# Strassen's first output and the gate's mix accumulated in PSUM, in a gated mix of linear attention and a Mish layer

## The chip, the cores and the metric

The kernel runs on one core of a Trainium2 chip. A core has five engines with a queue each: TensorE (PE in the profile, its weight loads PEld) multiplies matrices into PSUM, VectorE (DVE), ScalarE (ACT) and GpSimd (POOL) work on tiles, and SyncE (SP) issues most of the DMAs. SBUF is the working memory of 128 partitions; PSUM has eight banks of 128 x 512 fp32 values, which the code names by three tags: "a" (three banks), "dn" (four) and "kv" (one). The metric is the device time of one execution in microseconds (us), the median of the runs.

## The reference

For x of 2048 rows and 512 columns it computes g * a + (1 - g) * b, with one gate g per row:

```python
g = sigmoid((x * gate_w).sum(-1, keepdims=True))
# a: q, k, v = x @ wqkv, 32 heads of 16
pq, pk = q @ w_phi, k @ w_phi                       # per head
phi = concat([softmax(p), softmax(-p)])             # of pq and of pk
kv, z = phi_k^T v, sum over rows of phi_k
a = (phi_q kv) / (phi_q z + 1e-6), heads joined, @ wo
# b: a dense layer with Mish
h = x @ w1 + b1
b = (h * tanh(softplus(h))) @ w2                    # 512 -> 1376 -> 512
```

All is fp32. The kernel multiplies in the type fp32r; each factor is split into a high part h and a rest l, and a product is h*h + h*l + l*h, so three matmuls stand for one.

## The kernel before, in words

**Stage A** (names A0 to A7) goes over eight chunks of 256 rows. It makes the k features (k0, k1 on TensorE; mx, mn, d0, d1, S, rS, ml on VectorE; E, the exponential, on ScalarE), sums kv and z, and makes q and v. For chunks 1 to 7, q and v come from Strassen's scheme in Winograd's form, with seven products p1 to p7 of six matmuls each in place of eight. **Stage S** makes the hidden layer: S0 for the row blocks 0 and 1, S1 for 2 and 3. Hidden columns are taken in five pairs of 128 (the digit behind the underscore is the pair's), and each pair is again seven products p1 to p7 over the two row blocks. **Stage B** (B0 to B3, 512 rows each) multiplies by w2 (dn0 to dn10, each a sweep of 12 matmuls over four row tiles), makes the q features, the numerator (nu), the product with wo (wo0 to wo3), and the mix.

**In a seven-product group**, p1 and p2 sum to the first output, and p1, p6, p7, p4 go one after the other into the same bank (`d["a"]`, `ps["a"]`), with a ScalarE copy of the bank between them where an output needs the sum so far: c1 after p1, c6 after p6. p2 has a bank of its own (`d["c"]`, `ps["c"]`), and a VectorE addition a2 adds that bank to c1's copy in SBUF (lines 423 and 740). p5 and p3 go into a third bank, which c5 copies. In stage S the sums then go through Mish on ScalarE (mA0, mA1, mB0, mB1); those of the first row block stay in SBUF, those of the second are stored to DRAM and read back (sB, la).

**The mix** of a row tile: for even blocks ScalarE scales the finished sweep (iz, out of the bank "dn" into SBUF), and VectorE adds g times the product with wo (fi, line 1058). For odd blocks ScalarE scales the product with wo (ag) and VectorE adds the sweep.

**What sets the order.** The text RUN is a list of step names written out by hand. It is run from left to right, and every instruction is pinned, so each engine's queue holds its instructions in that order. An engine takes its queue in order: an instruction that waits holds up all behind it. SyncE's queue of DMAs is such a queue too. Buffers rotate by tag: the n-th tile of a tag gets buffer n modulo the number of buffers, and waits until that buffer's last reader is done.

**The low parts** are subtractions of raw and high part: on GpSimd for sl (line 368), wd (line 700), the rest of wo (WL, line 586), most of x (line 628), the h of the sweeps (line 824) and w2 (gl, line 559). gh (ScalarE) makes the high part of a pair's w2 blocks from raw tiles that lg loads.

Of the kernel before, what the change touches and what calls it, by code (L numbers as in the profile page):

```python
# [8 lines left out]
F32 = mybir.dt.float32  # L9
# [31 lines left out]

RUN = """
    A0.mx0 A0.mx1 A0.xh A0.xl A0.v0 A0.mn1 A0.mn0 A0.fq A0.fh2 S0.l11 A0.d10 A0.tA0 A0.fh1 A0.v1 A0.tA1 A0.tH1 A0.fl1 A0.tB1 A0.tB0 A0.fl2 A1.p1
    A0.ve1 A0.d11 A0.tH2 A0.fh0 A0.fl0 A0.d00 A0.d01 A0.tL1 A0.tL2 A0.fh3 A0.fl3 A0.E0 A0.E1 A2.lx A0.tC3 A0.tC4 A0.tH4 A1.k0 A1.mn0 A0.q0 A0.qe0
    A1.su A1.c1 A1.mx0 A1.d10 A1.ldx A0.tH3 A1.p2 A1.d00 A0.S1 A0.S0 A1.E0 A1.S0 A0.ldx A0.tL4 A0.q1 A1.xh A1.xl A1.k1 A1.mx1 A0.rS1 S0.l21 A1.rS0
    A0.qe1 A2.p1 A0.rS0 A0.tL3 A1.sh A2.k0 A1.ml0 A2.k1 A1.d01 A0.ml0 A1.a2 A2.p2 A1.sl A1.p6 A2.su A1.mn1 A1.d11 A0.ve0 A1.E1 A2.xh A0.ml1 A2.xl
    A0.st0 A0.st1 A0.z1 A1.c6 A0.z0 A1.z0 S0.h21 A2.c1 A1.p5 A0.kv A1.c5 A1.S1 A1.rS1 A1.p7 A1.p3 A2.sh A2.sl A3.su A2.mn0 A1.ml1 A1.a7 A2.mx1 A1.st1
    A3.k1 A2.a2 A1.a3 A2.mx0 A2.d10 A2.d00 A3.p1 A2.E0 A2.S0 A3.ldx A2.rS0 A1.z1 S0.wr_0 A2.p6 A2.c6 A2.ldx A2.p5 A2.c5 A2.p7 A1.p4 A2.d01 A2.mn1
    A2.d11 A2.E1 A2.p3 A3.sh S0.wa_0 A2.ml0 A1.st0 A3.mn1 A3.c1 A3.k0 A2.a3 A2.z0 A2.st0 A3.sl A3.p5 A2.a7 A2.p4 A1.e4 A3.xh A2.S1 A3.mx0 A3.mx1
    A3.mn0 A1.kv A3.xl S0.l12 A2.e4 A2.rS1 A2.ml1 A2.kv A3.d00 A3.d10 A3.E0 S0.wb_0 S0.ws_0 A3.p6 A4.p1 A2.z1 A3.d11 A3.S0 A3.rS0 A3.ml0 A2.st1 A2.wx  # L50
    A3.c5 A4.k0 A4.mn0 A3.c6 A4.su A3.p3 A4.d10 A3.a3 A4.c1 A3.p7 A4.sh A4.mx0 S0.h11 A4.d00 A3.a7 A4.k1 A4.E0 A3.st1 A3.d01 A4.mn1 A4.d11 A4.S0 A4.sl
    A3.p2 A3.a2 A4.mx1 A4.p5 A4.p6 A3.z0 A3.E1 A4.xh A4.c6 A4.ldx A3.S1 A3.rS1 A4.p2 A4.p7 A4.d01 A4.c5 A3.ml1 A3.p4 A4.a7 A4.st1 A4.E1 A3.st0 S0.o11
    A4.xl A4.rS0 A4.ml0 A4.p3 A5.su A5.sh A4.a3 A3.z1 S0.t1 A3.e4 B0.lq0 A5.k0 A5.k1 A5.mx0 A4.S1 A4.z0 A4.rS1 A4.ml1 A5.sl S0.h1 S0.o1 A4.z1 S0.o21
    A5.xh A5.p1 A5.c1 A3.kv A5.p5 A5.c5 A4.st0 A4.a2 A5.mn0 A5.p6 A5.mx1 A5.xl A5.d01 S0.wc_0 A5.mn1 A5.d10 A5.d11 A5.d00 A5.E0 A4.p4 A5.S0 A5.rS0
    A5.p3 A6.p1 A5.E1 A6.su A5.c6 A5.ml0 A5.z0 B0.mx0 A5.a3 A4.e4 A5.p7 A6.sh A6.sl A5.S1 A5.rS1 A4.kv B0.mn0 A5.ml1 A5.ldx A6.xh A6.k0 A6.mn0 A6.mx0
    A5.a7 A6.d00 A6.d10 A6.k1 A6.mn1 A6.mx1 A6.E0 A5.p2 A5.st0 A5.z1 A6.S0 A6.c1 A6.p2 A6.a2 S0.l22 A5.p4 A6.d01 A5.st1 A6.p6 A6.d11 A6.p5 A6.xl
    A6.rS0 A6.ml0 A6.c6 A6.p7 A7.su A6.E1 A6.S1 A6.c5 A6.p3 A5.e4 S0.t2 A6.z0 S0.fr0 A5.a2 A6.rS1 A7.p1 A6.a7 A7.p2 A7.sh A6.zr A7.sl A6.st1 A6.p4
    A6.ml1 S0.h2 S0.t3 S0.fh0 S0.t4 A7.k0 S0.h22 A6.z1 S0.fl0 S0.o22 A6.e4 A7.mn0 A6.a3 A5.kv A6.kv A7.c1 S0.lg1 A7.d10 A7.mx0 A7.d00 B0.d00 A6.zm
    S0.o2 A7.p5 A7.E0 A7.S0 A7.rS0 A6.st0 A7.c5 A7.k1 A7.mx1 A7.mn1 S0.gh1 S0.gl1 S0.wr_1 S0.h3 S0.p1_0 A7.d01 A7.p6 A7.c6 A7.d11 A7.p3 A7.ml0 A7.E1
# [47 lines left out]
def tile_gated_mix(ctx: ExitStack, tc: tile.TileContext, xT, wv, wkT, wqT, bd, w1a, w1b, b1, w2a, w2b, wo, out):  # L107
# [8 lines left out]

    def mm(*a, **k):
        return pin(nc.tensor.matmul(*a, **k))  # L118

    def T(shape, dt, tag, bufs, name):  # L120
        nm[0] += 1
        return sp.tile(shape, dt, name=f"{name}_{nm[0]}", tag=tag, bufs=bufs)
# [23 lines left out]
    def f32(ap):  # L146
        return ap.bitcast(F32)
# [1087 lines left out]
```

## Time and profile before

| what | value |
|---|---|
| median of 3 runs | 430.3 us (429.46 to 431.18) |
| the profiled execution, first to last instruction | 431.1 us |
| the slowest of the three runs | 431.18 us |
| TensorE (PE) busy | 422.3 us, 98% |
| VectorE (DVE) busy | 369.3 us, 86% |
| ScalarE (ACT) busy | 253.6 us, 59% |
| GpSimd (POOL) busy | 263.6 us, 61% |
| mean granted TensorE clock | 0.996 |

A busy time is the union of an engine's instructions. Matmuls are pipelined: one of 128x512 lasts 389 ns in the records, but the next starts 227 ns after it, so PE's busy share alone doesn't tell how close TensorE is to its pace. In a row of the timeline the first number is the start in us from the span's start, the second the duration, and a bracket at the end tells how long the engine had been idle and what ended that. L118 and L138 are the helpers through which every matmul and nearly every ScalarE instruction is recorded, so groups are told apart by tiles.

### The profile page before, as it was taken

The numbers are of one execution on the slowest core, as the hardware profiler recorded it, in microseconds if no ns is written. First come the engines' busy times: TensorE is split into PE (matmuls) and PEld (weight loads), VectorE is DVE, ScalarE is ACT, GpSimd is POOL, SyncE is SP. The second block draws the span as 40 slices with busy tenths as digits, with TensorE's granted clock in tenths as the row PEclk, the third lists the DMA queues.
The fourth block names the chain that finished last, engine by engine and source line by source line (L and its number), as shares of the span: only waits on it lengthen the run. The fifth ranks groups of instructions, "written<-read, shape, count | busy, mean of one in ns | idle before, by whom it ended". The sixth has DMA issues, their size and how long they took to land. (4 is left out here: it accounts for less than half of the span.)

```text
span 431.1 us, 7558 instructions
## 1 busy us (share of the span) xinstructions
PE 422.3 (98%) x2772; PEld 340.2 (79%) x2772; DVE 369.3 (86%) x519; ACT 253.6 (59%) x373; POOL 263.6 (61%) x186
## 2 busy tenths in 40 slices
PE   8999999999998999899999999999999999999996
PEld 7888888888886877688878687788788887877875
DVE  3899789998998999998999998799989699999512
ACT  3574463646254899768679813467978467851131
POOL 2298868799674966635666494977455627541220
PEclk9999999999999999989999999999999999999999
DMA  7900597675988344433888477833533725555532
GB/s 260 366 34 28 164 273 182 140 179 126 209 171 214 108 134 123 160 109 122 235 249 281 165 239 237 281 91 122 177 119 143 232 73 188 179 199 168 197 121 75
DMA packets 52670, 74.06 MB, mean 172 GB/s; under 512 B 8085, under 2 KB 32149, under 8 KB 52633
## 3 DMA queue, kind: packets, MB, share of 16 engines
q1 hardware_dynamic: 50440, 66.36, 47.9%
q0 software_dynamic: 1904, 6.82, 9.5%
q8 instruction: 22, 0.36, 0.3%
q10 hardware_dynamic: 288, 0.39, 0.3%
q14 instruction: 16, 0.12, 0.1%
HBM read 43.53 MB, written 28.85 MB: 168 GB/s over the span
## 5 line engine op out<-in xcount | busy, mean ns | idle before, releaser
L118 PE MATMUL down<-w2g,h 128*128 128x512 f32 x316 | 98.5, 393 | 0.0
L118 PEld LDWEIGHTS down<-w2g,h 128*128 128x128 f32 x316 | 58.6, 188 | 14.8 <-issue 2.5
L118 PE MATMUL down<-w2g,l 128*128 128x512 f32 x158 | 61.8, 391 | 0.2 <-POOL l L824 0.2
L824 POOL TENSOR_TENSOR l<-act,h 128x512 fp32r<-128x512 f32 (+1 forms) x24 | 32.3, 1345 | 41.2 <-ACT h L138 16.7
L824 POOL TENSOR_TENSOR l<-actb,h 128x512 fp32r<-128x512 f32 x20 | 29.0, 1451 | 38.3 <-ACT h L138 20.7
L138 ACT ACTIVATE E<-E 128x1024 f32<-128x1024 f32 x32 | 33.4, 1057 | 16.5 <-DVE E L285 7.1
L118 PE MATMUL up<-x,w1sh 128*128 128x512 f32 x144 | 39.7, 397 | 2.2 <-DVE act L740 2.1
L118 PE MATMUL wo<-woh,ohl 128*128 128x512 f32 x128 | 40.9, 389 | 0.0
L118 PEld LDWEIGHTS down<-w2g,l 128*128 128x128 f32 x158 | 29.6, 188 | 7.5 <-POOL l L824 1.2
L118 PEld LDWEIGHTS up<-x,w1sh 128*128 128x128 f32 x144 | 26.7, 189 | 9.2 <-DVE act L740 2.5
L700 POOL TENSOR_TENSOR w1sl<-w1r,w1sh 128x1024 fp32r<-128x1024 f32 x9 | 22.2, 2467 | 18.0 <-ACT w1sh L138 17.4
L118 PE MATMUL proj<-tw,sx 128*128 128x512 f32 x126 | 31.5, 394 | 1.5 <-ACT qs L138 1.5
L628 POOL TENSOR_TENSOR x<-xr,x 128x1024 fp32r<-128x1024 f32 x10 | 26.7, 2666 | 3.6 <-ACT x L138 3.6
L118 PEld LDWEIGHTS proj<-tw,sx 128*128 128x128 f32 x126 | 23.3, 188 | 6.9 <-ACT qs L138 1.9
L138 ACT ACT_TABLE_LOAD x22 | 28.2, 1283 | 0.4
L118 PEld LDWEIGHTS wo<-woh,ohl 128*128 128x128 f32 x128 | 24.0, 188 | 5.0
L138 ACT ACTIVATE act<-act,b1s 128x512 f32<-128x512 f32 x30 | 21.4, 719 | 10.9 <-DVE act L740 4.1
L118 PE MATMUL up<-x,w1d 128*128 128x512 f32 x108 | 27.7, 398 | 0.0
L267 POOL TENSOR_TENSOR xl<-xraw,xh 128x512 fp32r<-128x512 f32 x14 | 18.3, 1370 | 15.3 <-ACT xh L138 15.0
L138 ACT ACTIVATE act<-up 128x512 f32<-128x512 f32 x30 | 17.6, 590 | 16.8 <-PE up L118 16.4
L138 ACT ACTIVATE h<-actb 128x512 fp32r<-128x512 f32 x20 | 12.4, 628 | 24.4 <-DMA actb<-ab 18.9
L118 PE MATMUL wo<-wol,ohl 128*128 128x512 f32 x64 | 24.9, 389 | 0.0
(173 smaller groups left out, 1086.4 us busy)
## 6 DMA issues: line engine op xcount, KB each, us to landing
ed<-E SPq DMA_DIRECT2D x16, 512.0 KB, 3.1
eT<-ed SPq DMA_DIRECT2D x64, 128.0 KB, 3.2
za<-E POOLq DMA_DIRECT2D x11, 512.0 KB, 6.8
xr<-in_xT_dram SPq DMA_DIRECT2D x20, 256.0 KB, 4.2
ab<-act SPq DMA_DIRECT2D x20, 256.0 KB, 2.9
actb<-ab SPq DMA_DIRECT2D x20, 256.0 KB, 3.3
pqd<-qs SPq DMA_DIRECT2D x16, 256.0 KB, 5.8
pq<-pqd SPq DMA_DIRECT2D x16, 256.0 KB, 3.6
```

The source lines that it names most:

```text
L118: return pin(nc.tensor.matmul(*a, **k))
L138: return pin(A_.activation(out_, in_, fn, **k))
L267: pin(eng.tensor_sub(xs[c][1][j], kt(rawx[c], SC)[:, 2 * j : 2 * j + 2, :], f32(xs[c][0][j])))
L628: pin((V if n in LOV else G_).tensor_sub(X[n][:, 1024:], xr[n], f32(X[n][:, :1024])))
L700: pin(G_.tensor_sub(W["sl"], W["r"], f32(W["sh"])))
L824: pin(G_.tensor_sub(U[i]["l"][:n, :], U[i]["a"][:n, :], f32(U[i]["h"][:n, :])))
```

## The change

1. **p2 is added in PSUM.** c1 now copies bank a to bank c, PSUM to PSUM, on ScalarE, and p2 accumulates onto it. The VectorE addition a2 is gone. In stage A a new ScalarE step e2 takes v out of bank c; in stage S Mish reads bank c directly.
2. **The mix is summed in PSUM** for blocks 0 to 2: iz scales the sweep from its "dn" bank into the bank of the product with wo, wo accumulates on it, and fi is a ScalarE copy to SBUF. g is multiplied into the q features' scale instead (sc). Block 3 keeps the old way with VectorE.
3. **The split wo** and the split w1 block of the gate's column are stored to DRAM once (WS, fs) and read back for S1 (and, for the w1 block, also for the second row block), in place of a new load, ScalarE copy and GpSimd subtraction.
4. **GpSimd's subtractions of 1024 columns** are two of 512 (low).
5. **RUN is another order,** and SLOTS gives each tile of most tags a buffer by number in place of the rotation.

The number of matmuls of each shape is the same.

```diff
+SLOTS = {
+    "a": (
+        "012001021202102101201021012212010202121010210212020210110211202101010101"
+    ),
...
+    def home(tag, bufs):
+        return (tag + next(homes[tag]), 1) if tag in homes else (tag, bufs)
...
+    def low(l, a, h):
+        for o in range(0, 1024, 512):
+            pin(G_.tensor_sub(l[:, o : o + 512], a[:, o : o + 512], f32(h[:, o : o + 512])))
...
-                    mm(acc[r // 64][c : c + 64, o : o + 64], staged[r : r + 64, k, G, c : c + 64], bds[r : r + 64, G, r : r + 64], start=True, stop=True, skip_group_check=True)
+                    mm(acc[r // 64][c : c + 64, o : o + 64], staged[r : r + 64, k, G, c : c + 64], bds[r : r + 64, G, r : r + 64], start=(fresh and G == 0), stop=True, skip_group_check=True)
...
         def sl():
-            pin(G_.tensor_sub(sx["t"][:, 1024:], rawx[c][:, :], f32(sx["t"][:, :1024])))
+            low(sx["t"][:, 1024:], rawx[c][:, :], sx["t"][:, :1024])
...
         def p2():
-            d["c"] = psum("proj", "dn")
-            product(d["c"], xq(0, 1), B((wvh, wvl), 1), True)
+            product(d["c"], xq(0, 1), B((wvh, wvl), 1))
...
         def c1():
-            vs[c, 0] = k2("v", "io")
-            act(vs[c, 0], d["a"])
+            d["c"] = psum("proj", "dn")
+            act(d["c"], d["a"])
...
-        def a2():
-            pin(V.tensor_add(vs[c, 0], d["c"], vs[c, 0]))
+        def e2():
+            vs[c, 0] = k2("v", "io")
+            act(vs[c, 0], d["c"])
...
+    def keep(dst, src):
+        pin(Sy.dma_start(dst, f32(src)))
+
+    def back(dst, src):
+        pin(Sy.dma_start(f32(dst), src))
...
             def p2():
-                ps["c"] = psum("up", "a")
-                product(ps["c"], ov(), Xv("21"), True)
+                product(ps["c"], ov(), Xv("21"))
...
-            def a2():
-                pin(V.tensor_add(v["A0"], ps["c"], v["A0"]))
+            def c1():
+                ps["c"] = psum("up", "a")
+                act(ps["c"], ps["a"])
...
-                pin(V.tensor_mul(sv, sv, d["d"][:, None, :].to_broadcast([P, 2, H])))
+                pin(V.scalar_tensor_tensor(sv, sv, g_sb[:, i : i + 1], d["d"][:, None, :].to_broadcast([P, 2, H]), op0=ALU.mult, op1=ALU.mult))
...
             def iz(t=t):
                 i = 4 * b + t
-                io[t] = k2("io", "io")
-                act(io[t], dn[t], scale=og_sb[:, i : i + 1])
+                num["wo", t] = psum("wo", ("kv", "a")[t % 2])
+                act(num["wo", t], dn[t], scale=og_sb[:, i : i + 1])
 
             def fi(t=t):
                 i = 4 * b + t
-                ps, s = (dn[t], og_sb) if b % 2 else (num["wo", t], g_sb)
-                pin(V.scalar_tensor_tensor(io[t], ps, s[:, i : i + 1], io[t], op0=ALU.mult, op1=ALU.add))
+                if b == NB - 1:
+                    pin(V.scalar_tensor_tensor(io[t], dn[t], og_sb[:, i : i + 1], io[t], op0=ALU.mult, op1=ALU.add))
+                else:
+                    io[t] = k2("io", "io")
+                    act(io[t], num["wo", t])
                 pin(Sy.dma_start(out[i * P : (i + 1) * P, :], io[t]))
```

Three places show what the order does. The first is ScalarE's queue in stage S0, around the copy c1 of pair 3. Before, the copy goes to SBUF (act_2049 out of up_2031); the two w2g_300 rows behind it are gh4.

```order
L138 ACTIVATE act_2006<-up_1861 128x512
L138 ACTIVATE act_1966<-act_1966,b1s 128x512
L138 ACTIVATE act_2049<-up_2031 128x512
L138 ACTIVATE w2g_300_2054<-raw_2045 128x512
L138 ACTIVATE w2g_300_2054<-raw_2047 128x512
L138 ACTIVATE act_1913<-act_1913,b1s 128x512
```

After the change the same copy is `up_2127<-up_2072`. The four w2g rows are gh3 and gh4, the row behind them Mish of pair 2 (mB1) and then the high part hi5.

```order
L195 ACTIVATE act_2082<-up_2023 128x512
L195 ACTIVATE w2g_303_2099<-raw_2095 128x512
L195 ACTIVATE w2g_303_2099<-raw_2097 128x512
L195 ACTIVATE w2g_304_2102<-raw_1844 128x512
L195 ACTIVATE w2g_304_2102<-raw_1846 128x512
L195 ACTIVATE act_2082<-act_2082,b1s 128x512
L195 ACTIVATE h_2117<-act_1930 128x512
L195 ACTIVATE up_2127<-up_2072 128x512
```

So four w2 copies, a Mish and a high part now stand ahead of a copy for which p2 of this pair waits. On TensorE, p1, p4 of pair 2 and that p2 stand like this after the change:

```order
L168 MATMUL up_2072<-x_990,w1d_2066 128x512 x6
L168 MATMUL up_1792<-x_1623,w1d_1703 128x512 x6
L168 MATMUL up_2127<-x_586,w1o_2067 128x512 x6
```

One product of six matmuls lies between p1 and p2 of the pair; before, p2 stood without a wait on ScalarE, into a bank of its own.

The second place is ScalarE's queue at the end of block 2 (B2), after the change: iz1 and iz0 fill the banks of wo1 and wo0, then come fi1 and fi0 (io rows), and iz2 and iz3 into the same two banks.

```order
L195 ACTIVATE wo_3923<-down_3191,og_sb 128x512
L195 ACTIVATE wo_3925<-down_3188,og_sb 128x512
L195 ACT_TABLE_LOAD
L195 ACTIVATE ge_sb<-ge_sb 128x4
L195 ACTIVATE h_3933<-actb_3931 128x512
L195 ACTIVATE h_3943<-actb_3941 128x512
L195 ACTIVATE E_3892<-E_3892 128x1024
L195 ACTIVATE io_3971<-wo_3923 128x512
L195 ACTIVATE io_3986<-wo_3925 128x512
L195 ACTIVATE wo_3989<-down_3194,og_sb 128x512
L195 ACTIVATE wo_3991<-down_3197,og_sb 128x512
```

Before, the four scalings of this block went to SBUF tiles and stood ahead of the products with wo or beside them; now the sweep's banks of tiles 2 and 3 come free only after the products with wo of tiles 0 and 1 have been copied out.

The third place is the end of TensorE's queue. Before, the last rows are the two half tiles `rest` of the last row tile:

```order
L118 MATMUL rest_4417<-w2g_300_2054,h_4289 128x256 x2
L118 MATMUL rest_4417<-w2g_300_2054,l_4291 128x256
L118 MATMUL rest_4417<-w2g_300_2054,h_4308 128x256 x2
L118 MATMUL rest_4417<-w2g_300_2054,l_4311 128x256
```

After the change they stand earlier, and the queue ends with the sweep's last two steps for a whole tile (df2):

```order
L168 MATMUL down_4004<-w2g_304_2102,h_4356 128x512 x2
L168 MATMUL down_4004<-w2g_304_2102,l_4358 128x512
L168 MATMUL down_4004<-w2g_304_2102,h_4258 128x512 x2
L168 MATMUL down_4004<-w2g_304_2102,l_4377 128x512
```

So the last tile that is mixed and stored is one of 512 columns in one DMA, and no longer two of 256 columns on two queues.

242 lines of the change are left out of this document (159 added, 83 removed).

## The prediction

> **What bounds the kernel now.** I read the page's first line, by which all work hides behind PE, and then the windows, to see where TensorE is not busy; their columns are the stretch, its length, then busy time of PE, PEld, DVE, ACT and POOL with counts, the granted TensorE clock, and the DMA share.
>
> ```profile
> PE 422.3 (98%) x2772; PEld 340.2 (79%) x2772; DVE 369.3 (86%) x519; ACT 253.6 (59%) x373; POOL 263.6 (61%) x186
> ```
>
> ```profile
> 80.00:120.00 40.00, 40.00 (x295) 32.78 (x294) 36.80 (x49) 18.53 (x27) 34.60 (x31) 1.00 0.78 174
> 120.00:160.00 40.00, 38.48 (x349) 31.07 (x347) 36.97 (x43) 27.29 (x42) 29.83 (x18) 1.00 0.62 153
> 160.00:200.00 40.00, 37.66 (x158) 29.85 (x155) 38.80 (x57) 30.91 (x45) 22.78 (x15) 0.96 0.38 120
> ```
>
> Only these two stretches around the change from stage A to stage S lose much: 1.52 us and 2.34 us of PE. Next I asked the list of waits who PE waited for (us in total, times, longest):
>
> ```profile
> PE up L118 <- DVE act L740: 2.1, 1, 2.1
> PE proj L118 <- ACT qs L138: 1.5, 1, 1.5
> PE warm L118 <- DVE ones L188: 1.1, 1, 1.1
> PE up L118 <- POOL w1sl L700: 0.3, 1, 0.3
> PE proj L118 <- DVE wkh L1094: 0.2, 1, 0.2
> PE down L118 <- POOL l L824: 0.2, 1, 0.2
> ```
>
> The third and fifth belong to the start, which the change doesn't touch. The other four make 4.1 us. For TensorE's pace I took a long run from the chain of waits, the groups for one matmul's own length, and the tail of the chain:
>
> ```profile
> 307.53 3.01 PE up L118 x12
> ...
> 319.37 6.80 PE up L118 x30
> ...
> 426.27 1.44 PE rest L118 x12
> 427.71 0.03 issue
> 427.74 0.48 DVE io L1050
> ```
>
> ```profile
> L118 PE MATMUL wo<-woh,ohl 128*128 128x512 f32 x128 | 40.9, 389 | 0.0
> ```
>
> A 128x512 matmul starts every 6.80 / 30 = 0.227 us and lasts 0.389 us. From 308 us to the tail the chain is one unbroken row of matmuls: **TensorE sets the time**, and since the change keeps every matmul, it can win only what PE loses by waiting. A wait costs 0.389 - 0.227 = 0.16 us more than the idle time shown, because the last matmul's tail is counted as busy: 4.1 + 4 x 0.16 = 4.75 us.
>
> There is one more loss. The timeline around the longest wait (start, duration, in brackets the idle time before and its releaser):
>
> ```profile
> 134.42 1.52 PE L118 MATMUL up<-x,w1d 128*128 128x512 f32 x6
> ...
> 176.35 1.74 POOL L559 TENSOR_TENSOR w2g<-raw,w2g 128x512 fp32r<-128x512 f32 x1
> 176.86 2.31 DVE L954 TENSOR_TENSOR T<-E,zb 128x1024 f32<-128x1024 f32 x1
> 179.10 1.21 DVE L958 TENSOR_REDUCE Dn<-T 128x64 f32<-128x1024 f32 x1
> 180.69 1.15 DVE L958 TENSOR_REDUCE Dn<-T 128x64 f32<-128x1024 f32 x1
> 181.77 0.67 DVE L740 TENSOR_TENSOR act<-up,act 128x512 f32<-128x512 f32 x1
> 182.49 1.62 PE L118 MATMUL up<-x,w1sh 128*128 128x512 f32 x4 [2.08 <-DVE act L740]
> 184.76 2.33 PE L118 MATMUL up<-x,w1d 128*128 128x512 f32 x6
> ```
>
> PE waits for the addition a2 (L740), which reads a PSUM bank that the next group needs and stands behind VectorE's feature work, one of it 2.31 us long beside a GpSimd subtraction. After the wait six matmuls take 2.33 us in place of 1.52: the window's granted clock is 0.96, so (1 - 0.96) x 40 = 1.6 us are lost to a slow clock as well. In all, 4.75 + 1.6 = 6.35 us can be won, and PE's own work leaves 431.1 - 6.35 = 424.7 us.
>
> The Trainium skill (TensorE: Matmul & The Clock Gate, "What's actually happening") has the clock halve only after an idle window of about 3.4 us. The trace does not agree: here 2.08 us of idle time was enough. By the page the shorter waits that I forecast below would never cost clock; by the row a new wait near 2 us can bring the 1.6 us back.
>
> **The change part by part.** Durations come from the groups:
>
> ```profile
> L138 ACT ACTIVATE act<-act,b1s 128x512 f32<-128x512 f32 x30 | 21.4, 719 | 10.9 <-DVE act L740 4.1 <-DVE act L746 4.0 <-DVE act L743 2.5
> L138 ACT ACT_TABLE_LOAD x22 | 28.2, 1283 | 0.4
> L138 ACT ACTIVATE x<-xr 128x1024 fp32r<-128x1024 f32 x16 | 16.7, 1052 | 4.3 <-POOL xr L621 1.6 <-PE proj L118 1.6 <-DVE xr L612 0.4
> L138 ACT ACTIVATE act<-up 128x512 f32<-128x512 f32 x30 | 17.6, 590 | 16.8 <-PE up L118 16.4 <-ACT h L138 0.4
> L368 POOL TENSOR_TENSOR sx<-xraw,sx 128x1024 fp32r<-128x1024 f32 x7 | 17.5, 2499 | 8.7 <-ACT sx L138 8.7
> L267 POOL TENSOR_TENSOR xl<-xraw,xh 128x512 fp32r<-128x512 f32 x14 | 18.3, 1370 | 15.3 <-ACT xh L138 15.0
> L138 ACT ACTIVATE w2g<-raw 128x512 fp32r<-128x512 f32 x10 | 6.0, 624 | 5.9 <-DMA raw<-in_w2a_dram 4.1 <-DMA raw<-in_w2b_dram 1.7
> L1061 DVE SCALAR_TENSOR_TENSOR io<-wo,g_sb,io 128x512 f32<-128x512 f32 x8 | 5.9, 736 | 0.1
> L138 ACT ACTIVATE io<-down,og_sb 128x512 f32<-128x512 f32 x8 | 5.2, 684 | 0.9 <-PE down L118 0.8
> ```
>
> *VectorE* loses 17 additions a2 of 0.67 us and 12 mixes of 0.74 us: 11.4 + 8.9 = 20 us of its 369. In 160:200 it was busy 38.80 of 40 us, and the longest wait hung on that queue. This wait goes: bank c is now freed by Mish on ScalarE. I take the whole 4.75 us of the four waits and the 1.6 us as removed. The bounds are 0 (a wait of the same length elsewhere, the first rival) and 6.35.
>
> *ScalarE* gets seven copies e2 (4.1 us). The mix takes 12 scalings of 0.68 and 16 copies of 0.59 where it took 16 scalings: +6.7. Three w1 copies of 0.62, two wo copies of 1.05 and two table loads of 1.28 go: -6.5. That is +4 us on 254, hidden in 41% of idle time as long as nothing waits for a single copy. That is where the cost is: **p2 now waits for c1.** The price of one copy from PSUM to PSUM is in no row; the nearest is 0.59 us (PSUM to SBUF), bounded by 0 and the 0.72 us of Mish from SBUF. With 0.16 us of matmul tail and two handovers (0.03 us each by the "issue" row), p2 needs 0.59 + 0.22 = 0.8 us between p1 and itself. The order leaves at least one product, 6 x 0.227 = 1.36 us. So c1 alone costs nothing, if ScalarE is free for it; the cover is 0.55 us, and any lateness of ScalarE beyond that lands on PE.
>
> The tightest place is pair 3 of S0 (the first place above). Ahead of c1 stand the four w2 copies, a Mish, a high part and c1 itself: 4 x 0.624 + 0.72 + 0.62 + 0.59 = 4.4 us. Their data come late: the raw tiles of gh3 reuse the buffers of gh2's, so the load waits for GpSimd's two subtractions gl2 (3.1 us with 1.53 each, my estimate from L267's 1.37 and the 1.74 in the timeline), these for gh2 (1.25). A w2 load lands in this time:
>
> ```profile
> raw<-in_w2a_dram SPq DMA_DIRECT2D x6, 256.0 KB, 7.4
> raw<-in_w2b_dram SPq DMA_DIRECT2D x5, 256.0 KB, 3.2
> out_dram<-io SPq DMA_DIRECT2D x15, 256.0 KB, 2.3
> out_dram<-io ACTq DMA_DIRECT2D x1, 128.0 KB, 1.7
> ```
>
> From gh2's start to p2: 1.25 + 3.1 + 3.2 + 4.4 = 12 us, and half a microsecond for issue and handovers. From p6 of pair 2, beside which gh2 stands in the order, to p2 of pair 3 TensorE has 60 matmuls, 13.6 us. One microsecond of slack, behind a queue that ran late before, is no safe cover. A new wait is bounded by 0 and by the 4.4 us (if the load lands only when p2 could start); I take 1.5, nearer to 0 since gh2 may also run early.
>
> *The mix.* At the end of block 2 the sweep of block 3 follows directly on wo0. Its tile 2 needs the bank that iz2 reads, iz2 needs the bank of wo0, and this is free after fi0: 0.59 + 0.68 + 0.2 = 1.5 us against the 6 matmuls (1.36 us) of tiles 0 and 1; iz3 is 0.68 us later, when tile 2 has taken 0.68. A wait of 0.15 to 0.4 us; I take 0.4, with bounds 0 and 1.4 (a 1.06 us exponential ahead of fi0). At the ends of blocks 0 and 1 other work lies between.
>
> *GpSimd.* 29 subtractions of 2.5 us become 58 of 1.37: +0.24 each, 7 us, and five of the w1 and wo kind go (3 x 1.4 + 2 x 2.8 = 9.8). It is not on PE's path for long, so 0. *DMAs*: the reloads replace loads of the same bytes; the stores WS and fs stand in SP's queue well after their data are made, so nothing behind them waits. 0. *The feature scale* with g is one VectorE instruction for another, 0. *SLOTS* removes waits for buffers, but no such wait is on PE's list except the bank already counted: 0.
>
> *The tail.* The last matmul is now followed by one mix of 0.74 us and one DMA of 256 KB (2.3 us) instead of 0.48 and 1.7: +0.26 + 0.6 = 0.86 us, with nothing to hide it.
>
> **Sum:** 431.1 - 6.35 + 1.5 + 0.4 + 0.86 = 427.5 us. The profiled execution is the slow end of the runs (431.18 against the median 430.3), and the spread of 1.7 us is about one slow-clock stretch, which this sum has already taken out; so I carry 427.5 over to the median unchanged: 0.65% faster. Less than 0.5%, 2.2 us, can't be told from no change here.
>
> **The rivals.**
>
> *The waits only change place* (430.7). The order is new at every step, and the old one too was fed to PE without a gap as far as matmul counts show; the four waits came from queues running late. If as much lateness returns without the slow clock: 424.7 + 4.75 + 0.4 + 0.86 = 430.7. For it: 8.9 of VectorE's 20 us are mixes, which come after the stage that stalls. Against it: the longest wait hung on a2 by name.
>
> *ScalarE's queue heads stop p2: slower* (435.8). The second wait on PE's list is of this kind already:
>
> ```profile
> 137.87 0.64 ACT L138 ACTIVATE w2g<-raw 128x512 fp32r<-128x512 f32 x1 [4.12 <-DMA raw<-in_w2a_dram]
> 138.40 1.04 ACT L138 ACTIVATE x<-xr 128x1024 fp32r<-128x1024 f32 x1
> 139.53 0.60 ACT L138 ACTIVATE qs<-proj 128x512 f32<-128x512 f32 x1
> 140.18 1.66 PE L118 MATMUL proj<-tw,sx 128*128 128x512 f32 x6 [1.52 <-ACT qs L138]
> ```
>
> ScalarE stood 4.12 us before a w2 copy that waited for its load, and a copy of a PSUM bank behind it held PE. In the new order gh1 stands ahead of the copies c1 of pairs 2 and 1, and gh3 ahead of pair 3's. If each waits as long as here, the first costs 4.12 less the 1.9 us of cover (two products less 0.8), 2.2 us, the second its bound of 4.4, and each wait over 2 us the 1.6 of clock: 424.7 + 0.4 + 0.86 + 2.2 + 4.4 + 3.2 = 435.8. It decides from new waits of 6.5 us on (432.5). Against it: the load above was of the slow w2a kind (7.4 us), gh3's is of the other (3.2), and two table loads fewer stand in the queue.
>
> *GpSimd gets late* (429.5). It was busy 34.60 of 40 us in 80:120. The Trainium skill (SBUF — State Buffer, "SBUF: two separate sides") says that of a VectorE instruction with two SBUF inputs and a GpSimd one whichever starts first holds the shared port to its end; then twice as many starts are twice as many chances for GpSimd to lose. By rows: a 1024-wide w1 subtraction took 2.40 or 2.88 us, so a lost start costs 0.5 us; with 0.24 and 0.5 for the five added instructions of such a stretch it has 3.7 us more to do and 5.4 to spare. PE would lose perhaps 2 us at the sx products, which leaves 429.5.
>
> ```profile
> 139.81 2.40 POOL L700 TENSOR_TENSOR w1sl<-w1r,w1sh 128x1024 fp32r<-128x1024 f32 x1
> 162.84 2.88 POOL L700 TENSOR_TENSOR w1sl<-w1r,w1sh 128x1024 fp32r<-128x1024 f32 x1 [4.57 <-ACT w1sh L138]
> ```
>
> **How the numbers follow.** Forecast 0.55, waits change place 0.17, ScalarE slower 0.18, GpSimd late 0.10. Faster: nearly all of the forecast and a third of the last, 0.55; slower: 0.18 and a quarter of the second, 0.22; the rest, 0.23, is no change. The low end is the sum without new waits, 424.7 + 0.86 = 425.5, less 0.5 for the spread of runs; the high end, 432.5, leaves out the worse part of the slower case. The forecast's own range is 425.5 to 428.5.
>
> **What would show it.** Right: in 120:200 PE is busy over 78 us at a clock of 1.00; the list of PE's waits has no VectorE addition of up, but a ScalarE copy into a bank of up or wo; VectorE is busy near 349 us; the time from the last matmul to the end is near 4.2 us, not 3.4. Wrong: PE waits of over 5 us in all, or a clock below 0.99 in any stretch, name the rival by the engine that they wait for.

## Result and the profile after

The changed kernel took 434.55 us in the median of four executions (434.11 to 436.16), the kernel before 430.74 (429.46 to 431.19): a ratio of 1.0108, 95% interval 1.0065 to 1.0151. The prediction was 427.5 us, 0.65% faster; the change is 1.1% slower by this ratio (0.9% by the medians), outside the predicted range. A second measurement (the run e6 below) gave 434.58 us and 1.0113 (1.0073 to 1.0153). In all later runs the kernel before spread far more than in its first four executions: 164 executions lie between 425.8 and 436.7 us, median 431.2. A ratio compares executions within 1.5% of each kernel's fastest, so it drops the slowest ones of the kernel before; the medians given with the runs are of all.

The first line of the changed kernel's page, and two of its windows (columns as in the prediction):

```profile
PE 424.3 (98%) x2772; PEld 338.6 (78%) x2772; DVE 353.7 (82%) x490; ACT 256.2 (59%) x385; POOL 257.0 (59%) x210
```

```profile
120.00:160.00 40.00, 40.00 (x353) 32.37 (x352) 34.83 (x43) 27.57 (x45) 30.01 (x25) 1.00 0.64 162
160.00:200.00 40.00, 40.00 (x178) 32.30 (x176) 37.83 (x61) 29.54 (x43) 25.73 (x20) 1.00 0.55 185
```

TensorE is busy 80 of 80 us at full clock where it was busy 76.1 before. The waits that carried the prediction are gone, and the list of TensorE's waits after has little that is new:

```profile
PE warm L168 <- DVE ones L249: 1.1, 1, 1.1
PE fuse L168 <- issue: 1.0, 1, 1.0
PE down L168 <- POOL l L923: 0.6, 1, 0.6
PE fuse L168 <- DMA bds<-in_bd_dram: 0.3, 1, 0.3
PE down L168 <- ACT h L195: 0.2, 1, 0.2
```

Yet the span grew from 431.1 to 432.4 us, and the last matmul starts at 427.42 us in both. Where did 5 us go? Three places. At the **start** the fusion of the query weights, now ahead of the values product, stops in its middle (timeline of PE):

```profile
14.02 0.93 PE L168 MATMUL fuse<-bds,wT 64*64 64x64 f32 x48
15.94 1.40 PE L168 MATMUL fuse<-bds,wT 64*64 64x64 f32 x80 [0.99 <-issue]
```

At the **end** one wide mix and one store follow the last matmul:

```profile
427.42 0.40 PE L168 MATMUL down<-w2g,l 128*128 128x512 f32 x1
427.91 0.75 DVE L1162 SCALAR_TENSOR_TENSOR io<-down,og_sb,io 128x512 f32<-128x512 f32 x1 [0.71 <-PE down L168]
```

From 427.82 to the end of the span are 4.62 us, where the kernel before had 3.43. And **all along**, the matmuls follow each other more slowly. Here is one unbroken stretch of down products in the timeline of the changed kernel, its first and its last matmul, 35 steps apart:

```profile
234.50 0.62 PE L168 MATMUL down<-w2g,h 128*128 128x512 f32 x2
...
242.66 0.40 PE L168 MATMUL down<-w2g,l 128*128 128x512 f32 x1
```

8.16 / 35 = 0.233 us per matmul, where the prediction took 0.227 for all of them. A slower step is no wait: PE counts as busy, at clock 1.00, and no list of waits shows it. From the records of all matmuls, the time from one start to the next, summed by kind, in the two profiled executions:

| start to start, us | before | after | difference |
|---|---|---|---|
| proj, up, down, wo: what steps over 0.26 us have beyond 0.227 (waits, slow clock, tails of groups) | 12.5 | 7.2 | -5.3 |
| proj, up, down, wo: the rest (mean step 227.1 and 229.6 ns) | 387.1 | 390.8 | +3.7 |
| fuse | 4.5 | 5.9 | +1.4 |
| warm, kvp, num, rest | 22.2 | 22.4 | +0.2 |
| last matmul's start to the end of the span | 3.7 | 5.0 | +1.3 |

### The profile page after: what moved, and what is told of

It reads as the page before. It is cut to its first block, busy times and chain, and to the rows that moved or that the text cites. A ratio compares the mean times of both kernels' runs of the same rounds, so it can differ in the third digit from the quotient of the medians.

```text
span 432.4 us, 7535 instructions
## 1 busy us (share of the span) xinstructions
PE 424.3 (98%) x2772; PEld 338.6 (78%) x2772; DVE 353.7 (82%) x490; ACT 256.2 (59%) x385; POOL 257.0 (59%) x210
## 4 chain that ended last, share of the span: by engine, by line
PE 96%; issue 2%; DMA 1%; POOL 0%; SPq 0%; DVE 0%; DVEq 0%; POOLq 0%
PE proj L168 29%; PE down L168 27%; PE up L168 25%; PE wo L168 10%; PE kvp L168 2%; PE num L168 2%; DMA wT<-in_wkT_dram 1%; PE fuse L168 1%; PE rest L168 0%; POOL l L923 0%; DVE io L1162 0%; SPq L235 0%; SPq L227 0%; DVEq L1162 0%; POOLq L923 0%
## 5 line engine op out<-in xcount | busy, mean ns | idle before, releaser
L168 PE MATMUL down<-w2g,h 128*128 128x512 f32 x316 | 99.9, 397 | 0.2 <-ACT h L195 0.2
L923 POOL TENSOR_TENSOR l<-act,h 128x512 fp32r<-128x512 f32 (+1 forms) x24 | 33.5, 1400 | 40.4 <-ACT h L195 27.3
L923 POOL TENSOR_TENSOR l<-actb,h 128x512 fp32r<-128x512 f32 x20 | 27.8, 1397 | 47.3 <-ACT h L195 37.4
L168 PE MATMUL up<-x,w1sh 128*128 128x512 f32 x144 | 38.6, 390 | 0.0
L199 POOL TENSOR_TENSOR w1sl<-w1r,w1sh 128x512 fp32r<-128x512 f32 x18 | 24.0, 1354 | 23.2 <-ACT w1sh L195 18.1
L199 POOL TENSOR_TENSOR x<-xr,x 128x512 fp32r<-128x512 f32 x20 | 28.2, 1447 | 3.8 <-ACT x L195 3.7
L1053 DVE TENSOR_TENSOR T<-E,zb 128x1024 f32<-128x1024 f32 x16 | 23.4, 1461 | 5.7 <-ACT E L195 5.4
L195 ACT ACTIVATE x<-xr 128x1024 fp32r<-128x1024 f32 x16 | 16.9, 1057 | 17.2 <-POOL xr L695 7.4
L421 POOL TENSOR_TENSOR xraw<-xraw 128x256 f32<-128x256 f32 x28 | 25.3, 905 | 1.9
L352 DVE TENSOR_REDUCE Sm<-E 128x64 f32<-128x1024 f32 x18 | 21.7, 1207 | 4.6 <-ACT E L195 4.6
```

What stands on the lines that cost most here:

```text
L195: return pin(A_.activation(out_, in_, fn, **k))
L199: pin(G_.tensor_sub(l[:, o : o + 512], a[:, o : o + 512], f32(h[:, o : o + 512])))
L352: pin(V.tensor_reduce(d["S"], hv(d["E"][:, :]), axis=AX.X, op=ALU.add))
L421: pin(G_.tensor_add(o, o, i))
L923: pin(G_.tensor_sub(U[i]["l"][:n, :], U[i]["a"][:n, :], f32(U[i]["h"][:n, :])))
L1053: pin(V.tensor_mul(d["T"], d["E"], B["zb"]))
```

## Experiments

Each run lists the median of its executions, their spread, and the ratio to the kernel before with its 95% interval.

**1. Where the tiles lie.** In the changed kernel every slot is a tag of its own, so tiles of 128 bytes lie between the large ones, and the slow matmuls were those whose moving operand starts 128 or 384 bytes past a multiple of 512 (places are those in the built programs). The run e1 gives the small tags their place first; nothing else changes.

```diff
+    for n, f in (("mx0", H), ("mx1", H), ("mn0", H), ("mn1", H), ("Sm0", 2 * H), ("Sm1", 2 * H)):
+        sp.tile([P, f], F32, name=f"first_{n}", tag=n, bufs=1)
     pqd = tc.dram_tile([S, D], F32, name="pqd")
```

> The changed kernel with the same program order and the same table of slots; the only difference is that the six small tags (mx0, mx1, mn0, mn1 of 128 bytes, Sm0, Sm1 of 256) get their place in SBUF ahead of all others, so that every tile of 2 KB and more starts at a multiple of 512 bytes, as in the kernel before. Theory 'placement' (the matmuls of the changed kernel follow each other at 229.6 ns instead of 227.1 because 618 of their moving operands start at 128 or 384 bytes past a multiple of 512): the mean pitch comes back to 227.1 to 227.5 ns, the last matmul starts some 3.7 us earlier in the span (423.7 instead of 427.4), and the time is 430.8 us (430.0 to 431.6). Rival 'order' (the matmuls are slower because of what the other engines do beside them in the new order, the halved GpSimd operations or the ScalarE copies in PSUM): the pitch stays at 229 to 230 ns and the time at 434.0 to 435.5 us.

Measured: 432.38 us (430.83 to 436.16), 1.0058 (1.0022 to 1.0093), mean step 227.2 ns. The stretch of down products shown above, in the timeline of e1:

```profile
233.87 0.62 PE L168 MATMUL down<-w2g,h 128*128 128x512 f32 x2
...
241.80 0.39 PE L168 MATMUL down<-w2g,l 128*128 128x512 f32 x1
```

7.93 / 35 = 0.227 us. The pitch came back as expected; the median time came back by 2.2 us and not 3.7, and missed its range. In the profiled execution other stops take 1.9 us back: the fusion, which now waits 1.3 us for its load before it begins, ends 0.5 us later than in the first profile; 0.5 us go at the sx products near 37 us, 0.4 at a wait for ScalarE near 314 us, the rest in smaller ones.

The run e2 shifts the whole pool of the kernel before by 128 bytes.

```diff
+    sp.tile([P, 32], F32, name="pad", tag="pad", bufs=1)
     pqd = tc.dram_tile([S, D], F32, name="pqd")
```

> The kernel before with one unused tile of 128 bytes ahead of its big pool: nothing else differs, and every tile of 2 KB and more now starts 128 bytes past a multiple of 512. Theory 'placement': all of the some 1,716 matmuls of 128x512 in proj, up, down and wo pay the 232.0 ns that the 618 shifted ones of the changed kernel show (only the first slice's down products, whose weights lie in another pool, do not), so 1,550 x 4.9 ns = 7.6 us more: 438.3 us (436.5 to 440). Rival 'order': 430.7 us, pitch 227.1 ns, since the order is that of the kernel before.

Measured: 432.31 us (427.37 to 436.85), 0.9999 (0.9950 to 1.0048), and 227.1 ns for 1,618 matmuls. The theory as stated fell: the absolute place costs nothing. But 27 matmuls whose moving operand lies in another pool, and had stayed behind, took 233.0 ns. So the distance between the two operands was left. (The run e3, a shift by 256 bytes, gave no time: the pool has no room for it.) The run e7 puts the same 128 bytes between the slots of hl and those of E, w2 and pq:

```diff
     new_x(0)
+    sp.tile([P, 32], F32, name="pad", tag="pad", bufs=1)
     pk = {}
```

> The kernel before with the unused 128-byte tile put between the slots of x, io, tx, m4, eT, z and hl and those of E, w2 and pq. The uniform shift by 128 bytes left the pitch at 227.1 ns and only the 27 matmuls whose moving operand had stayed behind took 233.0. New theory 'relative placement': a matmul is some 5.5 ns slower when its moving operand and the weights that are loaded beside it start 128 bytes apart (modulo 256). Here 483 matmuls of down and 90 of proj become so, about as many as in the changed kernel (469 and 89); up and wo do not. Expected: down at 232.5 ns where it was 227, up at 227.1, a mean of 229.0, and 575 x 5.4 ns = 3.1 us more time than the kernel before. Rival 'order': no change of pitch, as with the uniform shift, since the order and the slots are those of the kernel before.

Measured: 432.67 us (429.83 to 436.49), 1.0038 (0.9989 to 1.0086); mean step 229.4 ns (229.0 expected), 493 matmuls with shifted moving operand and unshifted weights at 232.7. The same stretch of one program, in e2 and in e7 (timelines, first and last of 36 matmuls):

```profile
256.45 0.62 PE L118 MATMUL down<-w2g,h 128*128 128x512 f32 x2
...
264.38 0.39 PE L118 MATMUL down<-w2g,l 128*128 128x512 f32 x1
```

```profile
253.28 0.62 PE L118 MATMUL down<-w2g,h 128*128 128x512 f32 x2
...
261.44 0.40 PE L118 MATMUL down<-w2g,l 128*128 128x512 f32 x1
```

7.93 against 8.16 us: one unused tile of 128 bytes makes the whole difference, in the old order. Relative placement is shown. Not all of it is in the shifted matmuls: those at equal places step at 227.9 ns in e7 and 228.0 in the changed kernel, where the kernel before has 227.1, some 0.9 us over 1,100 of them. Why they slow down too is not shown. The price of the placement in time is hidden in e7, because the kernel before spreads so far: the fastest execution of e7 is 429.83, of the kernel before beside it 426.44.

**2. Both kernels again.** The runs e5 and e6 are the two kernels unedited.

> The kernel before itself, unedited, to have its spans and times beside each other on the chip of this group. In the four runs of the changed kernel the time was 1.66 to 1.75 us above the span of the same execution. If that holds for the kernel before too, the profiled execution of before that the prediction was built on (span 431.1 us) took some 432.8 us, slower than every listed run (429.46 to 431.19), and its slow-clock stretch is not in the median. Theory 'base': the time is again 1.7 us above the span, and the span of a typical run is 428.5 to 429.5 us, without the slow clock. Rival: time and span of before agree within 0.3 us as 431.18 and 431.1 suggest.

Measured: 430.92 us (427.35 to 433.83), 0.9996; its profiled execution took 431.78 us with a span of 430.1, so 1.7 us lie outside the span here too. By that the profile on which the prediction stood is of an execution of some 432.8 us, 2 us above the median. A median execution then spans 429.2 us, as the theory had it. In e5's profile the slow clock is absent and the waits at 140 and 183 us are there.

> The changed kernel itself, unedited, on the same chip as the others of this group: the ratio to before as first measured, 1.0108 (1.0065 to 1.0151), and a pitch of 229.6 ns again, as its addresses are the same. If the pitch comes back at 227.2 ns, or the ratio within 0.3% of 1, the first result was the chip's and not the kernel's.

Measured: 434.58 us (433.73 to 437.80), 1.0113 (1.0073 to 1.0153), step 229.5 ns. The slowdown is the kernel's. But in this profiled execution, of the same program, the fusion at the start ran through, in 4.6 us where the first profile has 5.9: that stop comes in some executions only.

**3. Start and end.** The run e4 has the small tags first, A0.v0 ahead of A0.fq, and B3.fi3 last. e8 moves ScalarE's fh0 to fh3 and VectorE's fl0 to fl3 up besides; e11 also fills VectorE's idle time ahead of them.

```diff
-A0.xl A0.fq A0.mn0 ... A0.tL2 A0.v0 A0.fl0
+A0.xl A0.v0 A0.fq A0.mn0 ... A0.tL2 A0.fl0
-B3.fi0 B3.fi3 B2.fi3 B3.wo2 ... B3.ag2 B3.fi2
+B3.fi0 B2.fi3 B3.wo2 ... B3.ag2 B3.fi2 B3.fi3
```

> The changed kernel with the small tags placed first (as in the first run of this group) and two steps of its order put where the kernel before has them: the values product of chunk 0 (A0.v0) ahead of the query fusion (A0.fq), and the last row tile's halves (B3.fi3) at the very end. Theory: beside the 3.7 us of the placement, the fusion no longer stops 0.99 us for the query weights and runs some 1.4 us shorter, and the tail from the last matmul to the end goes from 4.6 to 3.4 us: 434.55 - 3.7 - 1.2 - 1.2 = 428.4 us (427.3 to 429.8), below both kernels. Rival (the ends are not on the path: another transfer or VectorE ends the span, or the query path waits for its weights in place of the fusion): 430.0 to 431.5 us, as with the placement alone.

> The changed kernel with the small tags placed first, B3.fi3 at the very end, and its start set anew: A0.v0 ahead of the query fusion as before, and now ScalarE's four copies of the fused query weights (fh0 to fh3) right behind the fusion, ahead of the copies tH1, ve1 and tH2, and VectorE's four subtractions (fl0 to fl3) in the same order. In the run with v0 moved alone the 0.99 us stop of the fusion went, but TensorE then stood 1.28 us for the copy wqh, which was queued behind these three. Theory: that wait goes, and the time is 1.3 us below that run, 430.4 us on the same scale (431.87 there), or some 0.3% below the kernel before. Rival (the values' copy ve1 and the tw copies that now come later stop A1.p1 or A1.p5 for as long): 431.5 to 432.5 us.

> The same kernel as in the run e8 (431.5 us), halves kept, with VectorE's feature work on chunk 0 (mn0, d10, mn1, d11, mx0, d00) in the 3.4 us in which it stood idle ahead of the fused query weights. In that run TensorE waited 0.51 us for the copy wql and 0.59 us for the bank that d00 reads. Theory: both waits go, 1.1 us, 430.4 us. Rival: the subtractions tA0 to tB0 come later and stop A1.p1 as long: 431.5 us.

Measured: e4 431.87 us (430.81 to 435.80), 1.0041 (1.0008 to 1.0074); e8 431.50 (430.98 to 432.36), 1.0049 (1.0016 to 1.0082); e11 431.93 (431.68 to 434.64), 1.0036 (1.0008 to 1.0064). All three expectations missed. In e4 the fusion ran through, and TensorE then waited for the copy wqh; with that gone in e8 it waited for wql and a bank; in e11 for the copies v and sx. The rivals came nearer, though e4 and e11 lie 0.4 us above theirs, and the waits are not all at the places that they named: the start is a chain of copies behind late weights, and the wait only changes its instruction. The end gave part: 4.3 us from the last matmul's start to the end of the span, in place of 5.0.

**4. GpSimd's halves.** The prediction gave them no cost and no gain. The run e9 makes them alone in the kernel before; e10 undoes them alone in the kernel of e8.

```diff
-pin(G_.tensor_sub(W["sl"], W["r"], f32(W["sh"])))
+low(W["sl"], W["r"], W["sh"])      # and likewise sl, lo of x (GpSimd's), wl
```

> The kernel before with one part of the change alone: GpSimd's subtractions of 1,024 columns (sl, lo of x, lo2, wl) in two halves. In the kernel before three profiled executions showed TensorE's waits at 140 and 182 us with VectorE operations of 2.3 and 3.4 us beside long GpSimd subtractions where 1.2 us is usual, and one (the relatively shifted tile) showed neither the waits nor those long operations; its times run from 426.4 to 434.6 us. Theory 'lock': the long VectorE operations last until a GpSimd subtraction beside them ends, so halving these shortens what VectorE stands still; the waits go or shrink, the times lie closer together and the median falls to 427.5 to 429 us. Rival 'order': the waits come from the order of VectorE's work and stay; 430 to 432 us, with as wide a spread.

Measured: 427.75 us (426.95 to 429.06), 0.9910 (0.9877 to 0.9942), and in the profiled execution TensorE waits for nobody after the start. That is the time that the theory 'lock' gave; e12 below shows that the waits do not always go.

> The changed kernel with small tags first and the new start and end (431.5 us, 430.98 to 432.36), with GpSimd's subtractions whole again. Prediction on record: the halves cost and bring nothing, so 431.5 us. Theory 'lock': TensorE's waits for VectorE or for what stands behind it come back in part, 433 to 435 us, with a wider spread of times.

Measured: 437.77 us (434.67 to 438.00), 1.0118 (1.0084 to 1.0153), 6.3 us above e8 and above both expectations. The first rows of TensorE's waits in e10:

```profile
PE proj L168 <- ACT qs L195: 1.8, 1, 1.8
PE proj L168 <- POOL sx L198: 1.2, 1, 1.2
PE warm L168 <- DVE ones L251: 1.1, 1, 1.1
PE wo L168 <- ACT wo L195: 1.1, 1, 1.1
PE up L168 <- POOL w1sl L198: 1.0, 2, 0.5
```

So the new order rests on the halves. Three waits, for sx, w1sl and w1e (0.6 us), are for GpSimd's results themselves. That TensorE can begin on a first half after 1.3 us instead of 2.4 fits, but is argued. The longest is for the copy qs, which stood 3.2 us for a store that landed late. And the wait for wo goes back to the lock between VectorE and GpSimd. On average VectorE's operations are hardly longer in e10 (the 16 products T take 1486 ns each, in e8 1442), but ahead of this wait, in e8 and then in e10, the timelines have

```profile
224.47 2.99 POOL L199 TENSOR_TENSOR wol<-raw,woh 128x512 fp32r<-128x512 f32 x2 [0.41 <-ACT woh L195]
224.92 1.39 DVE L349 TENSOR_TENSOR E<-pq,mx 128x512 f32<-128x512 f32 x1
```

```profile
229.01 2.40 POOL L198 TENSOR_TENSOR wol<-raw,woh 128x1024 fp32r<-128x1024 f32 x1 [0.56 <-ACT woh L195]
229.05 2.90 DVE L348 TENSOR_TENSOR E<-pq,mx 128x512 f32<-128x512 f32 x1
```

VectorE's operation ends only after GpSimd's has, 1.5 us later with the whole subtraction than with halves, and TensorE waits 1.1 us for ScalarE's copy wo, which stands behind VectorE's next results. The Trainium skill (SBUF — State Buffer, "SBUF: two separate sides") describes this lock: the instruction that starts first holds the shared port to its end. The rows agree, and experiment 5 has a second case.

The runs e12 (e9 again) and e13 (e9 with the 128 bytes of e7) were to give the price of the placement in a kernel without waits.

> The kernel before with GpSimd's subtractions of 1,024 columns halved, once more and beside the next run on the same chip: 427.75 us as in the first run (426.95 to 429.06), a ratio to before near 0.991, no wait of TensorE over 0.3 us beyond the bias matmuls of hc.

> The same kernel with the unused tile of 128 bytes between hl and the slots behind it, so that 575 matmuls have their moving operand 128 bytes (modulo 256) away from the weights loaded beside it. TensorE waits for nobody in this kernel, so the pitch alone decides. Theory 'relative placement': 493 measured matmuls at 232.7 ns and the others near 227.5, 575 x 5.4 ns = 3.1 us: 430.8 us (430.3 to 431.5). Rival (the slower pitch is a matter of the records' modelled ends and starts and no time, or is made good in waits): 427.5 to 428.2 us.

Measured: e12 428.65 us (426.89 to 432.41), 0.9961 (0.9926 to 0.9997); e13 433.81 (430.03 to 434.44), 1.0059 (1.0018 to 1.0100). The fastest differ by 3.1 us, as expected; the medians differ by 5.2, and both expectations missed. For both profiled executions have the waits at 140 and 180 us: the halves do not remove them. The steps up to 0.26 us sum to 391.0 us in e13 and 387.3 in e12, 3.7 us more.

**5. What the old waits were.** e9 and e12 are the same program, and every engine keeps step within 0.1 us from 23 to 135 us. Then ScalarE's queue (timeline; e9 first, then e12):

```profile
133.82 0.62 ACT L138 ACTIVATE w2g<-raw 128x512 fp32r<-128x512 f32 x1
135.36 0.63 ACT L138 ACTIVATE w2g<-raw 128x512 fp32r<-128x512 f32 x1 [0.91 <-DMA raw<-in_w2a_dram]
```

```profile
133.78 0.62 ACT L138 ACTIVATE w2g<-raw 128x512 fp32r<-128x512 f32 x1
139.03 0.63 ACT L138 ACTIVATE w2g<-raw 128x512 fp32r<-128x512 f32 x1 [4.63 <-DMA raw<-in_w2a_dram]
139.57 1.04 ACT L138 ACTIVATE x<-xr 128x1024 fp32r<-128x1024 f32 x1
140.52 0.58 ACT L138 ACTIVATE qs<-proj 128x512 f32<-128x512 f32 x1
```

The same load of w2, issued at 130 us, lands late, and the copy qs for which TensorE waits stands behind it. The landing of the four loads between 118 and 152 us, from the view of the tile raw, in e9 and in e12:

```profile
DMA to landing us min/median/max: 2.6/4.7/6.2
```

```profile
DMA to landing us min/median/max: 6.5/7.5/8.5
```

The run e14 takes the copy behind qs in the kernel before, e15 in the halved one.

```diff
-... S0.gh1 S0.gl1 S0.wr_1 S0.h3 S0.p1_0 A7.d01 A7.p6 A7.c6 ...
+... S0.wr_1 S0.h3 S0.p1_0 A7.d01 A7.p6 A7.c6 S0.gh1 S0.gl1 ...
```

> The kernel before with one step moved: the copy of w2's second group (S0.gh1, and GpSimd's S0.gl1 with it) from ahead of S0.wr_1 to behind A7.c6, so that the copy qs no longer stands behind a copy that waits for a load. Theory 'late load': the wait of some 1.5 to 2 us at 140 us goes in every execution, and with it part of VectorE's lateness at 160 to 185 us; the median falls from 431 to 428 to 429.5 us. Rival 'lock' (VectorE beside GpSimd sets the waits): the wait at 140 us may go, but the waits at 166 and 182 us stay, 430 to 431 us.

> Both: GpSimd's subtractions halved and the same step moved. Theory 'late load' with the halves as a second, smaller gain: no wait of TensorE in any execution, times close together at 426.8 to 428 us, a ratio to before near 0.991. Rival (the load that lands late stops something else, the weights of the w2 products or GpSimd's subtractions of them): 428.5 us with the spread of the halved kernel (426.9 to 432.4).

Measured: e14 435.64 us (432.77 to 438.13), 1.0101 (1.0053 to 1.0149); e15 433.28 (430.64 to 435.57), 1.0033 (1.0004 to 1.0061). Both missed: slower. ScalarE in e14 shows why the wait at 140 us stays (1.2 us):

```profile
138.97 0.60 ACT L138 ACTIVATE qs<-proj 128x512 f32<-128x512 f32 x1 [4.43 <-DMA pqd<-qs]
```

Now qs itself waits, for a store of the same moment; besides, TensorE waits 2.1 us for GpSimd's w1sl. So transfers in both directions are late, and what runs beside them is an accumulation of 512 KB on GpSimd's queue, issued at 131 us (DMA view of e12, 122 to 142 us; last column median us to landing):

```profile
raw<-in_w2a_dram SPq DMA_DIRECT2D x4, 256.0 KB, 7.5
zacc<-za POOLq DMA_DIRECT2D x1, 512.0 KB, 8.2
```

The runs e16 (kernel before) and e17 (halved) leave it out, and with it that part of the feature sums.

```diff
-            at(key, "zm", lambda: pin(G_.dma_start(zacc, za[0], accum_op=ALU.add)))
+            at(key, "zm", lambda: None)
```

> The kernel before without the one step A6.zm: the accumulating transfer of 512 KB that adds za[0] to zacc is left out, so the feature sums of the global attention lack that part, and nothing else changes. Theory 'late landing': the four loads of w2 and the store of qs at 129 to 136 us land in 2.5 to 5 us, the wait of TensorE at 140 us goes in every execution and with it most of those at 166 and 182 us: 427 to 428.5 us, times close together. Rival 'lock': those at 166 and 182 us stay, 430 to 431.5 us, as wide a spread as before.

> The kernel with halved subtractions without the same step A6.zm (its sums lack the same part). Theory 'late landing': no wait of TensorE, 426.5 to 427.5 us in every execution. If the halves bring nothing of their own once the load is in time, the time is the same as that of the kernel before without the step; theory 'lock' expects the halved one 2 to 3 us below it.

Measured: e16 426.55 us (425.70 to 429.20), 0.9942 (0.9909 to 0.9974); e17 427.12 (426.34 to 428.99), 0.9961 (0.9932 to 0.9991). In e16 the four loads land early, and all that TensorE waits for is:

```profile
DMA to landing us min/median/max: 2.7/3.6/4.7
```

```profile
PE warm L118 <- DVE ones L188: 1.1, 1, 1.1
PE down L118 <- POOL l L824: 0.2, 1, 0.2
```

In e17's profile it is the same, and without the transfer the halves bring nothing. So the late loads, and with them the wait at 140 us, hang on this transfer. The Trainium skill (DMA: Bandwidth & Descriptors, "Queues, rings and completion order") lets each DMA engine take turns between queues packet by packet; later landings beside a second queue agree with it.

The complete kernels e18 and e19 issue the transfer after A7.z0 instead.

> The kernel before, complete, with the accumulating transfer A6.zm moved from 131 us on GpSimd's queue to behind the addition A7.z0, which ended at 142 to 144 us, that is after the w2 loads of 129 to 136 us and before the addition A7.z1 that needs it. The transfer took 8.6 us, z1 began at 149.5 to 151.4 us, so z1 and the transpose behind it may come 1 to 3 us later. Theory 'late landing': the wait at 140 us goes, 427 to 428.5 us in nearly every execution. Rival (it delays others wherever it stands, the loads and stores issued from 141 to 150 us now): waits at 150 to 175 us, 429.5 to 432 us.

> The kernel with halved subtractions and the same move of A6.zm. By the run without the transfer (427.1 halved, 426.55 whole) the halves bring nothing once the load is in time: 427 to 428.5 us, as the run beside it; if the halves still bring 2 us, 426 to 426.5 us.

Measured: e18 429.45 us (428.39 to 433.62), 1.0035 (0.9995 to 1.0075); e19 428.65 (427.98 to 429.39), 0.9994 (0.9960 to 1.0027). Both lie above the expected 427 to 428.5. The wait at 140 us went, one for a VectorE addition at 180 us stayed (2.1 us in e18, 0.9 in e19), so that one does not follow from the first. It goes back to the lock. Around 167 us VectorE's product T and a GpSimd subtraction begin almost together, in e16 and then in e18:

```profile
167.19 1.21 DVE L954 TENSOR_TENSOR T<-E,zb 128x1024 f32<-128x1024 f32 x1
167.48 3.20 POOL L700 TENSOR_TENSOR w1sl<-w1r,w1sh 128x1024 fp32r<-128x1024 f32 x1 [0.76 <-PE up L118]
```

```profile
166.93 2.51 POOL L700 TENSOR_TENSOR w1sl<-w1r,w1sh 128x1024 fp32r<-128x1024 f32 x1 [0.31 <-PE up L118]
167.09 3.43 DVE L954 TENSOR_TENSOR T<-E,zb 128x1024 f32<-128x1024 f32 x1
```

The one that starts first takes its usual time, the other is held up until it has ended. In e18 two more VectorE operations are held up at once, beside the subtractions of w2 (1.72 and 2.31 us in place of 0.67 and 1.21), so the addition a2 starts at 179.30 us and not at 175.05. All 13 profiles of the kernel before and its variants divide so: in e7, e9, e16 and e17 T starts first and TensorE does not wait at 180 us; in the other nine GpSimd starts first, by 0.1 to 0.5 us, and TensorE waits, 2.1 us with whole subtractions and 0.7 to 0.9 with halves. So profiles e16 and e17 alone do not show that the transfer makes this wait. What puts one or the other first was not tried. The transfer still costs 1.5 to 3 us (e19 against e17, e18 against e16); the spread of e19, 1.4 us, is with that of e8 the smallest of all kernels with every part of the work.

**The better kernel** is the one before with GpSimd's subtractions halved and nothing else of the change: 427.75 and 428.65 us, ratios 0.9910 and 0.9961, both intervals below 1, and 6 to 7 us below the changed kernel.

## Why the prediction was wrong

From 427.5 to 434.55 are 7.05 us: 1.7 of the base, 4.95 of steps within the span, 0.4 between the profiled execution after (434.15) and the median.

- **"SLOTS removes waits for buffers, but no such wait is on PE's list: 0"** and the pitch of 0.227 us, carried over without a word: +3.7 us. This is the step that failed most. The table moved tiles, some 560 matmuls got operands 128 bytes apart modulo 256, and each took some 5.5 ns more than the 227.1 of before (3.0 us); the others took some 0.8 ns more. The view of the chain showed the pitch before; nothing in it said what the pitch depends on.
- **The start, not costed:** +1.4 us in the profiled execution, nothing in e6's, so how much of it is in the median is not known. The order put the fusion ahead of the product that had covered the load of its weights. The difference of the orders showed this; I looked at three places and not there.
- **"GpSimd: 0."** The halves are not neutral: 6.3 us in the new order (e10 against e8), 2.4 to 3.4 in the old one by medians. That is a gain the sum did not have, eaten by the rest. The rival that let GpSimd get late had the lock, but with the other loser: here VectorE stood still, and halves shorten the wait at 180 us by 1.2 to 1.4 us.
- **The tail:** 0.86 forecast, 1.19 measured, right in kind, +0.33.
- **The four waits and the slow clock:** 6.35 us less 1.9 of new waits forecast, a net 4.45; measured 5.3. The new waits at pair 3 and at iz2 did not come (the rival of ScalarE's queue heads fell with them), but 0.6 us for GpSimd's l did. The size was right and the reason wrong. The prediction laid the longest wait to the addition a2; e16 shows the same waits gone with a2 in place, and what makes a2 late is the order in which VectorE and GpSimd start at 167 us (experiment 5). In the changed kernel no w2 load is issued between 122 and 142 us, which fits, though the order was not tried alone. Nor does the slow clock follow from the wait's length: the same wait of 2.1 us left the clock at 1.00 in e2, e5, e14 and e18. The rule of an idle window of some 3.4 us (the Trainium skill, TensorE: Matmul & The Clock Gate, "What's actually happening") would not have it start there either. What differs is where the idle time lies. The clock's changes in the traces stand whole multiples of 3.413 us after its first rise, 5.56 us in this execution, and the half clock lasts one such stretch (windows of PE; the figure behind the count is the clock):

```profile
179.64:183.05 3.41, 1.33 (x6) 1.00 0.36 115
183.05:186.46 3.41, 3.41 (x9) 0.50 0.81 253
```

The whole 2.08 us lie in the stretch before the fall; in e2, e5, e14 and e18 a stretch ends inside the wait, and none holds more than 1.87 us of it. That fits, but one fall in 20 profiles does not prove it.
- **"I carry 427.5 over to the median unchanged."** The span of 431.1 was set beside a time of 431.18 as if they were one execution. Time is some 1.7 us above span in every execution that has both (1.66 to 1.97). So the base was 432.8, and 2.1 us of what the change was to win were not in the median of 430.7 at all: those waits come in some executions and not in others.
- **The signs to watch for** came true where they carried the forecast (TensorE over 78 us busy in 120:200, no a2 in its list, clock 1.00) while the time went the other way. The others did not: no ScalarE copy into up or wo is in the list, VectorE is busy 353.7 us and not 349, the end takes 4.6 us and not 4.2. None of them looked at the step from one matmul to the next.

What is left when placement, start and end are put right (e8, span 429.4) still lies 4.1 us above the halved kernel without waits (e9, span 425.3): 2.2 us in proj, 0.5 in up, 0.5 in down, 0.8 in num and wo, 0.6 in the tail, less 0.5 in fuse. Which of it is the copies in PSUM and which the order was not separated.

## What to carry to other kernels

Before trusting that a pace stays, compare the addresses of the operands in the two kernels: a change that only renames buffers can slow every matmul, and no list of waits shows it, only the time from start to start. Take more than one profile of a kernel whose times spread: a wait that comes in some executions only is not in the median in full, and an edit cannot win all of it there. And when a queue's head waits for a load, look at what else moves at that moment before moving the copy. Where a VectorE operation takes twice its usual time, look at what GpSimd began just ahead of it.

## What was not expected of the hardware

- A 128x512 matmul whose moving operand and the weights loaded beside it start 128 bytes apart modulo 256 follows after 232.6 ns (543 matmuls of e6, 547 of e7), where equal places give 227.1 (e2, both shifted by 128) and places 256 bytes apart 228.0 (161 matmuls of e6, in which equal places have 228.0 too).
- One accumulating transfer of 512 KB on GpSimd's queue took loads of 256 KB on SP's queue from 2.7 to 4.7 us to as much as 8.5 us, in some executions and not in others.
- Less than half a microsecond decides which of two operations is held up: VectorE's T took 3.43 us when GpSimd's subtraction began 0.16 us ahead of it (e18), and 1.21 when T began 0.29 us ahead (e16).
- Time and span differed by 1.66 to 1.97 us in every execution that has both, most in e10.
